# Instruction orders taken from a list schedule, five column blocks per ring, and block-diagonal kv weights, in an attention and channel-mix kernel

## The chip, the cores and the metric

The kernel runs on one core of a Trainium2 chip. The metric is the device time of one execution in microseconds (us), the median over repeated runs. A profiled execution also gives a span, from the first to the last instruction; where the record pairs the two, the span is about 1.7 to 2.1 us shorter than the time.

Engines are named as in the profile: PE is TensorE (PEld its weight loads), DVE is VectorE, ACT is ScalarE, POOL is GpSimd, SP is SyncE.

## The reference

There are 8 batches, 8 heads, 576 rows and head size 64. The attention has no score matrix: `exp(k)` is normalised over the sequence, `exp(q)` over the head size, and the kv matrix is 64 by 64 per head. The result goes into a channel mix with 1,024 hidden columns.

```python
q_s = exp(q - max);  q_s = q_s / sum(q_s, over head_dim)
k_s = exp(k - max);  k_s = k_s / sum(k_s, over seq)
x   = q_s @ (k_s.T @ v)                  # per head, then [batch, seq, 512]
x_prev = x shifted by one row
xk = mu_k*x + (1-mu_k)*x_prev;  xr = mu_r*x + (1-mu_r)*x_prev
out = sigmoid(xr @ w_r) * (relu(xk @ w_k)**2 @ w_v)
```

## The kernel before

Work comes in 16 attention groups (a batch and half of its heads) and in units of the channel mix. A group needs three loads of 576 KB (q, k, v), three operations on ScalarE, a row sum and a scaling of q on VectorE, kv products, nine transposes and two x products on TensorE, and then `xk` and `xr` on VectorE. A unit multiplies up to 512 columns of `xk` and `xr` by the weights. The kernel works in pairs of batches, with three units per pair, and mixes the two kinds of work by a rule that counts columns:

```python
UNITS = ((0, 512), (512, 384), (896, 256))           # per pair of batches
...
first = emit_load(0, 0, (nc.sync, nc.scalar, nc.sync))   # q, k, v of group 0
...                                                      # then the two small mu loads on nc.sync
emit_load(0, 1, (nc.scalar, nc.sync, nc.scalar))         # q, k, v of group 1
emit_weights(first[2])      # weight loads on GpSimd wait for group 0's v
...
def weights(self):                                   # kv weights of one group
    for hf in range(2):
        nc.vector.reciprocal(out=rz[:, hf:hf + 1], in_=self.kvp[hf][:, 128:129])
    for hf in range(2):                              # 128 x 128, off-diagonal blocks masked away
        nc.vector.scalar_tensor_tensor(
            out=self.w[:, hf, :], in0=self.kvp[hf][:, 0:128],
            scalar=rz[:, hf:hf + 1], in1=mask[:], op0=ALU.mult, op1=ALU.mult)
...
for pair in range(B // 2):
    for c0, n in UNITS:
        advance(ASTEPS * (2 * pair + (c0 + n - 1) // S))
        for c in unit(pair, c0, n, 4 if pair == 0 and c0 == 0 else 1):
            cols += c
            advance(min((B - 1) * ASTEPS, ASTEPS * (cols + per_batch // 8) // per_batch))
```

The softmax here doesn't subtract the row's maximum and nothing guards it: scores larger than these inputs give would overflow.

## Time and profile before

| | before |
|---|---|
| time, median (range) of three runs | 221.07 us (221.0 to 221.58) |
| profiled span | 219.7 us |
| matmul work, counted at the start-to-start time of back-to-back matmuls at full granted clock | 181.5 us |
| dense matmuls start | 27.8 us |
| TensorE time lost from there (27.8–40, 40–60, 60–160, from 160) | 1.9 + 2.9 + 4.7 + 1.0 us |
| tail after the last matmul | 4.75 us |

The work row is not the profile's busy time. In this trace matmuls of 512 columns start 0.216 us apart, and the 144 of L284 have a mean recorded duration of 0.379, so their records overlap. So matmuls are counted here by their start-to-start time (0.216 us at 512 columns), and "lost" is the stretch minus that work. "Warm" in the prediction means that rate: from 27.7 to 31.1 us, where this trace has a granted clock of 0.50, matmuls of 512 columns start 0.427 us apart.

The first lines are from the page of before: busy times, the span in 40 slices of 5.5 us (busy tenths; PEclk is the granted clock in tenths), and the chain of work that ended last, by engine.

```profile
PE 193.5 (88%) x1313; PEld 101.6 (46%) x1313; DVE 166.3 (76%) x384; ACT 147.7 (67%) x230; POOL 35.8 (16%) x56
...
PE   0156599988999999999999999999999999999991
...
DVE  1196389999999998889798998888787758483431
ACT  2645279999977779676929696949736392644340
...
PE 60%; ACT 19%; DVE 13%; DMA 3%; issue 2%; SPq 1%; DVEq 0%; ACTq 0%
```

TensorE is dense from about the sixth slice. VectorE is full up to about 85 us and ScalarE up to 60. The table of windows says it in numbers (columns: window, its length, then busy us and number of instructions of PE, PEld, DVE, ACT, POOL, then granted clock, DMA share and GB/s):

```profile
40.00:60.00 20.00, 18.34 (x141) 9.58 (x140) 19.93 (x45) 20.00 (x29) 8.31 (x12) 1.00 1.03 400
60.00:80.00 20.00, 19.92 (x140) 10.71 (x139) 19.79 (x46) 15.16 (x26) 4.95 (x7) 1.00 0.94 348
80.00:100.00 20.00, 19.41 (x121) 9.28 (x120) 17.39 (x36) 15.31 (x22) 4.24 (x6) 1.00 0.71 242
100.00:120.00 20.00, 19.81 (x161) 11.82 (x159) 17.52 (x42) 15.46 (x27) 2.12 (x3) 1.00 0.54 186
```

After 80 us VectorE has over 2 us free in each window of 20.

The head, from the timeline of before (columns: start, duration, engine, line, operation, output and inputs, count, and in brackets the idle time before it and what ended it):

```profile
5.97 2.22 ACT L154 ACTIVATE eqk<-raw 128x1152 bf16<-128x1152 f32 x2 [2.17 <-DMA raw<-in_q_dram]
...
9.79 0.24 PE L134 MATMUL mup<-identf,mu_sb 8*128 8x8 f32 x1 [9.79 <-DMA mu_sb<-in_moe_mu_r_dram]
...
10.16 1.34 DVE L166 TENSOR_REDUCE rsum<-eqk 128x18 f32<-128x1152 bf16 x1
...
13.25 1.14 PE L202 MATMUL qtp<-ident,qs 128*128 128x128 bf16 x9 [1.52 <-DVE qs L170]
...
27.82 1.01 PE L270 MATMUL kfp<-xk,wk_bf 128*128 128x512 bf16 x2 [2.92 <-DVE xk L232]
```

The first q has landed at 5.97 us, but its row sum starts only at 10.16. In the order of VectorE's instructions the copy of mu stands in front of it, and that copy starts at 10.07, after VectorE has been idle for 8.52 us: it waits for the transpose at 9.79, which waits for the small mu load.

### The profile page before, as it was taken

Reading aid. Unit: us, or ns where it says so; the run is one execution under the profiler, and the core shown is the slowest. Engines: PE = TensorE matmul, PEld = TensorE weight load, DVE = VectorE, ACT = ScalarE, POOL = GpSimd, SP = SyncE. Lnnn points to the kernel's source line nnn. Section 1 sums busy time; section 2 is a strip of 40 time slices with the busy share of each in tenths; the row PEclk is TensorE's granted clock in tenths of the full one; section 3 lists DMA queues with packets and bytes.
Section 4 is the critical chain, followed back from the end, with each engine's and each line's share of the span. In section 5 each row is a group of like instructions: output and inputs, shape, how many; then the busy total and the mean of one; then the engine's idle time right before and its main releaser. Section 6 shows DMA issues by size and latency. Waiting matters only on the chain.

```text
span 219.7 us, 3641 instructions
## 1 busy us (share of the span) xinstructions
PE 193.5 (88%) x1313; PEld 101.6 (46%) x1313; DVE 166.3 (76%) x384; ACT 147.7 (67%) x230; POOL 35.8 (16%) x56
## 2 busy tenths in 40 slices
PE   0156599988999999999999999999999999999991
PEld 0134134534547454445557443546465444554650
DVE  1196389999999998889798998888787758483431
ACT  2645279999977779676929696949736392644340
POOL 1294252433431210230030000000000000000000
PEclk9999969999999999999999999999999999999999
DMA  6999999999999791897085220232131400340414
GB/s 215 397 158 199 262 402 388 393 400 403 404 393 406 273 343 71 256 298 288 3 264 201 49 51 0 57 90 48 36 88 24 95 3 22 73 95 5 108 36 95
DMA packets 16171, 40.62 MB, mean 185 GB/s; under 512 B 2072, under 2 KB 4632, under 8 KB 16152
## 3 DMA queue, kind: packets, MB, share of 16 engines
q0 software_dynamic: 8736, 27.40, 38.0%
q1 hardware_dynamic: 6600, 11.22, 18.0%
q10 hardware_dynamic: 816, 1.77, 2.2%
q8 instruction: 10, 0.16, 0.3%
q14 instruction: 9, 0.07, 0.1%
HBM read 33.56 MB, written 9.44 MB: 196 GB/s over the span
## 4 chain that ended last, share of the span: by engine, by line
PE 60%; ACT 19%; DVE 13%; DMA 3%; issue 2%; SPq 1%; DVEq 0%; ACTq 0%
PE vp L291 22%; PE kfp L270 19%; PE rp L284 11%; ACT eqk L154 5%; ACT qt L207 4%; ACT rel L276 4%; DMA mu_sb<-in_moe_mu_r_dram 3%; PE kvp L184 3%; PE qtp L202 3%; PE xp L212 2%; DVE rsum L166 2%; DVE xk L232 2%; DVE qs L170 2%; ACT xb_105 L215 2%; ACT xb_109 L215 1%
## 5 line engine op out<-in xcount | busy, mean ns | idle before, releaser
L270 PE MATMUL kfp<-xk,wk_bf 128*128 128x384 bf16 (+2 forms) x384 | 72.6, 335 | 4.3 <-DVE xk L232 3.7
L276 ACT ACTIVATE rel<-kfp 128x512 bf16<-128x512 f32 (+2 forms) x96 | 45.4, 518 | 20.5 <-PE kfp L270 19.5
L270 PEld LDWEIGHTS <-wk_bf 128*128 128x128 bf16 x384 | 36.3, 99 | 30.3 <-issue 8.5
L154 ACT ACTIVATE eqk<-raw 128x1152 bf16<-128x1152 f32 x32 | 37.5, 1204 | 9.7 <-DMA raw<-in_q_dram 5.9
L294 DVE SCALAR_TENSOR_TENSOR ot<-th,vp 128x512 f32<-128x512 f32 x36 | 24.6, 683 | 17.3 <-PE vp L291 12.5
L287 ACT ACTIVATE th<-rp 128x512 f32<-128x512 f32 x36 | 22.7, 631 | 21.7 <-PE rp L284 20.7
L284 PE MATMUL rp<-wr_bf,xr 128*128 128x512 bf16 x144 | 37.0, 379 | 0.0
L207 ACT COPY qt<-qtp 128x1152 bf16<-128x1152 bf16 x16 | 18.2, 1136 | 7.7 <-PE qtp L202 7.5
L166 DVE TENSOR_REDUCE rsum<-eqk 128x18 f32<-128x1152 bf16 x16 | 21.6, 1348 | 1.6 <-ACT eqk L154 1.5
L170 DVE TENSOR_TENSOR qs<-eqk,rrec 128x1152 bf16<-128x1152 bf16 x16 | 21.7, 1355 | 0.8
L230 DVE TENSOR_SCALAR xm<-xd,mu 128x576 bf16<-128x576 bf16 x64 | 21.6, 378 | 0.4
L284 PEld LDWEIGHTS <-xr 128*128 128x128 bf16 x144 | 13.3, 98 | 13.8
L72 POOL DMA_DIRECT2D raw<-in_q_dram x14 | 10.0, 713 | 52.9 <-ACT vv_111 L160 24.0
L212 PE MATMUL xp<-qt,w 128*128 128x512 bf16 x64 | 13.5, 302 | 2.6 <-ACT qt L207 2.3
L184 PEld LDWEIGHTS <-eqk 64*128 64x128 bf16 x288 | 9.4, 100 | 9.2 <-issue 8.3
L202 PE MATMUL qtp<-ident,qs 128*128 128x128 bf16 x144 | 11.6, 231 | 1.5 <-DVE qs L170 1.5
L202 PEld LDWEIGHTS <-qs 128*128 128x128 bf16 x144 | 9.8, 103 | 4.1 <-DVE qs L170 1.8
L212 PEld LDWEIGHTS <-w 128*128 128x128 bf16 x64 | 6.3, 103 | 11.0 <-issue 6.1
L72 POOL DMA_DIRECT2D raw<-in_v_dram x14 | 10.0, 711 | 8.4 <-DMA raw<-in_q_dram 5.8
L72 POOL DMA_DIRECT2D raw<-in_k_dram x14 | 10.0, 711 | 5.7 <-DMA raw<-in_v_dram 3.0
L195 DVE SCALAR_TENSOR_TENSOR w<-kvp,rz,mask 128x128 bf16<-128x128 f32 x32 | 9.7, 345 | 0.0
L134 PE MATMUL mup<-identf,mu_sb 8*128 8x8 f32 x1 | 0.2, 243 | 9.8 <-DMA mu_sb<-in_moe_mu_r_dram 9.8
(83 smaller groups left out, 238.7 us busy)
## 6 DMA issues: line engine op xcount, KB each, us to landing
out_dram<-ot SPq DMA_DIRECT2D x72, 128.0 KB, 2.4
raw<-in_q_dram POOLq DMA_DIRECT2D x14, 576.0 KB, 12.4
raw<-in_k_dram POOLq DMA_DIRECT2D x14, 576.0 KB, 12.7
raw<-in_v_dram POOLq DMA_DIRECT2D x14, 576.0 KB, 13.1
wk_bf<-in_moe_w_k_dram POOLq DMA_DIRECT2D x4, 256.0 KB, 6.5
wv_bf<-in_moe_w_v_dram POOLq DMA_DIRECT2D x2, 512.0 KB, 12.4
raw<-in_k_dram ACTq DMA_DIRECT2D x1, 576.0 KB, 5.6
raw<-in_q_dram SPq DMA_DIRECT2D x1, 576.0 KB, 5.2
```

The costliest lines, as they stand in the source:

```text
L72: ld.append(queue.dma_start(out=t[:, i, :, :], in_=ap))
L154: nc.scalar.activation(out=self.eqk[:, i, :, :, :], in_=self.t[:, i, :, :].rearrange("p u (j d) -> p j u d", d=D), func=ACT.Exp)
L166: nc.vector.reduce_sum(out=rsum[:], in_=eq, axis=AX.X)
L170: nc.vector.tensor_tensor(out=self.qs[:].rearrange("p j (u d) -> p (j u) d", u=2), in0=eq, in1=rrec[:, :, None].to_broadcast((128, 2 * J, ...
L202: nc.tensor.transpose(out=self.qtp[:, j, :], in_=self.qs[:, j, :], identity=ident[:])
L207: nc.scalar.copy(out=self.qt[:], in_=self.qtp[:, 0:J, :])
L212: nc.tensor.matmul(self.xp[:, 64 * c:64 * e], lhsT=self.w[:, hf, :], rhs=self.qt[:, c:e, 64 * hf:64 * hf + 64], start=True, stop=True)
L270: nc.tensor.matmul(kfp[:, 0:n], lhsT=wk_bf[:, ct, fc * 128:(fc + 1) * 128], rhs=xk[:, ct, c0:c0 + n], start=(ct == 0), stop=(ct == CT - 1))
L276: nc.scalar.activation(out=rel[:, 0:n], in_=kfp[:, 0:n], func=ACT.Relu, scale=HALF_ROOT)
L284: nc.tensor.matmul(rp[:], lhsT=xr[:, ct, c0 + 128 * m:c0 + 128 * m + 128], rhs=wr_bf[:, ct, :], start=(ct == 0), stop=(ct == CT - 1))
L291: nc.tensor.matmul(vp[:], lhsT=k2[:, ft, 128 * m:128 * m + 128], rhs=wv_bf[:, ft, :], start=(ft == 0), stop=(ft == FT - 1))
L294: nc.vector.scalar_tensor_tensor(out=ot[:], in0=th[:], scalar=1.0, in1=vp[:], op0=ALU.add, op1=ALU.mult)
```

## The change

The intent is to replace the hand-made mixing rule by a schedule. Every operation is registered with its engine, the time that it occupies the engine (`occ`), its latency (`lat`), a priority key, its inputs and the buffers it takes and gives. A list scheduler then goes through them in simulated time, and the kernel emits each engine's instructions in the order of that plan. Four batches share a ring of 2,304 columns cut into five units instead of six, and the kv weights are written as two 64-partition diagonal blocks into a zeroed tile.

```diff
-    UNITS = ((0, 512), (512, 384), (896, 256))                       # per 2 batches
+    UNITS = ((0, 512), (512, 512), (1024, 512), (1536, 512), (2048, 256))   # per 4 batches
...
+class Plan:
+    def order(self):
+        while left:                       # simulated time, all engines
+            ...
+                    rank = (max(t, now + 0.03), op.key)      # t: when op could start
+            ...
+            if op.size:                   # loads: one stream of 395 KB/us
+                dma_free = max(dma_free, t + DMA_LEAD) + op.size / DMA_RATE
+                op.end = dma_free + DMA_TAIL
...
-    first = emit_load(0, 0, (nc.sync, nc.scalar, nc.sync)) ... mu ... emit_load(0, 1, ...)
-    emit_weights(first[2])                                   # weights wait for the first v
+    first = [load("SP", 0, 0, 0, 0), load("ACT", 0, 0, 1, 0), ...]
+    mu_load = plan.add("SP", 0.8, 0.8, 2, emit_mu_load, size=4.0)
+    wk_done.append(plan.add("POOL", 1.25, 1.25, h, ..., [], size=1048.0))    # no wait
...
-            for hf in range(2): nc.vector.reciprocal(...)            # 2 reciprocals
-            for hf in range(2): nc.vector.scalar_tensor_tensor(... in1=mask[:] ...)
+        def recz():                                                  # 1 reciprocal
+            nc.vector.reciprocal(out=rzs[w.index][:, :, None], in_=atts[kvp.index][:, :, 128:129])
+        def weights():
+            for u in range(2):
+                r = slice(64 * u, 64 * u + 64)
+                nc.vector.tensor_tensor(
+                    out=ws[w.index][r, :, r], in0=atts[kvp.index][r, :, r],
+                    in1=rzs[w.index][r, :, None].to_broadcast((64, 2, 64)), op=ALU.mult)
...
+        o = plan.add("DVE", 0.066, 0.15, step + 4, recz, [kvm], [w])
+        wdone = plan.add("DVE", 0.5, 0.6, step + 4, weights, [o], [], [kvp])
...
+    for op in plan.order():
+        op.emit()
```

In the resulting order the SyncE queue issues the mu loads first, then the first group's q. The first weight loads on GpSimd wait for nothing.

## The prediction

> **What bounds the kernel now.** TensorE, counted by work, not busy time. In the timeline, warm back-to-back matmuls start every 0.216 us at 512 columns, 0.163 at 384, 0.109 at 256; 18 kv products take 0.63 us, nine transposes 0.50. [...] Summed over all matmuls it is 181.5 us of the 219.7 us span. Lost, by 20 us windows of start times: 17.6 us before 20, 7.1 in 20-40, 2.9 in 40-60, 5.7 from 60 to 215, and 4.5 in the tail (last output operation and store). So 25 us are lost before dense matmuls run (27.8 us and shortly after); at most 8.6 can be won after 40.
>
> **What the change does.**
> 1. TensorE work stays: ten K units cost 62.2 us against 62.4.
> 2. VectorE: kv weights go from two reciprocals and two masked operations (0.84 us per group in the timeline) to one reciprocal and two 64-partition blocks, estimated 0.65: 3 us in 16 groups; fewer squares: 1 us. Off the critical path except in 40-80, where VectorE is 99% busy.
> 3. Body: ScalarE is busy 20.0 of 20 us in 40-60 while TensorE waits for its copies; the new orders spread this. Loss after 40 us: from 8.6 to about 4.
> 4. Head, better: mu loads go first. Before, mu landed at 9.65 us and held the first row sum until 10.16, though its exponential was done by 7.1.
> 5. Head, worse: the weight loads on the GpSimd queue no longer wait for the first v, so they start near 2.8 us and compete with the six first loads. By packets in the trace, the two hardware queues move about 85 each per us alone; in 11-12 us, when the weights join, the three move 64, 61 and 49[...]. At 60 packets per us a 256-packet load takes 4.3 us, not 3. Estimate: first q at 7.1 us (5.97 before), second group's q at 11.5, last of the six near 16 (12.7 before). ScalarE now takes the second group's q before the first's, so it waits to 11.5. Walking the new order with the old durations: first row sum 12.8, first xk 27, second xk 32, so dense matmuls begin at 30-32 us instead of 27.8: plus 2 to 4. Weights land 3 us earlier, batch 1's first q at 28 instead of 28.95.
>
> **Sum.** 31 us head + 176.5 remaining matmul work + 2 lost in the first unit + 2.5 later + 4.5 tail = 216.5 us. Predicted 216.5 us, 8 in 10 between 211.5 and 221. Faster by over 2% 0.47, within 2% 0.48, slower 0.05.
>
> **What would show it.** In the chain of waits and the timeline: the first row sum at 12-13 us, waiting for a DMA through ScalarE's exponential; dense K matmuls from 30-32 us; under 1 us lost per 20 us window after 60; the same last 4.5 us; weight packets from about 3 us, the six first loads landing by 16. VectorE busy falls by 3-6 us, with no effect of its own.
>
> **What would make it wrong.** If the weights do not slow the first loads, dense work starts at 27-28 us and the time is 211-213. If the fixed order meets waits that its durations did not foresee (two attention PSUM slots), the body keeps its losses and the time stays at 220.

31 + 176.5 + 2 + 2.5 + 4.5 is 216.5 us. The 0.216, 0.163 and 0.109 us, and the 64, 61 and 49 packets, are from the trace of before; that three queues would move 60 each for longer is the estimate from the latter. The 0.65 us of the new kv weights is a forecast of a form that had not run yet; in after it took 0.695 us from start to start.

## The result

After ran in 224.09 us (224.05 to 224.81, four runs), before in 221.03 us on the same chip (four runs, the three above and one more). The ratio is 1.0133, with a 95% interval of 1.0108 to 1.0159. A ratio here is the mean time of one kernel's fast runs over that of the other's in the same rounds, so it is not quite the ratio of the medians. The prediction's range ended at 221; the change costs 1.3%.

| | before | predicted | after |
|---|---|---|---|
| dense matmuls start | 27.8 | 31 | 30.2 |
| matmul work from there | 176.6 | 176.5 | 176.2 |
| TensorE time lost from there | 10.6 | 2 + 2.5 | 11.0 (1.5 before 40, 4.0 in 40–60, 5.3 in 60–160, 0.1 later) |
| tail | 4.75 | 4.5 | 4.75 |
| span | 219.7 | | 222.1 |
| time (before: its median; after: that run) | 221.07 | 216.5 | 224.11 |

Against before, the span is 2.4 us longer, and dense matmuls start 2.4 us later. From there on after loses 0.4 us more and has 0.4 us less to do. So the head cost about what it was expected to cost (partly by luck, as told below), and the gain that was expected of the body did not come. The granted clock is no rival: its mean was 0.990 in the profile of before and 1.000 in that of after.

The page of after, the same parts:

```profile
PE 190.5 (86%) x1249; PEld 95.2 (43%) x1249; DVE 159.7 (72%) x350; ACT 147.5 (66%) x214; POOL 35.9 (16%) x56
...
PE   0036569996799899999999989999999999999991
...
DVE  1271798999999999999999999999432442342431
ACT  4357259999999998999996662783452362372340
...
PE 54%; DVE 35%; DMA 4%; issue 3%; ACT 2%; SPq 0%; DVEq 0%
```

VectorE has 6.6 us less to do, and yet its share of the chain rose from 13% to 35%. The row of tenths says why: the list schedule takes attention work as early as it can, so VectorE shows nines without a gap until slice 28 (about 155 us) and ones to fours after that. In the windows:

```profile
40.00:60.00 20.00, 16.85 (x138) 8.32 (x137) 19.48 (x39) 20.00 (x26) 8.50 (x12) 1.00 1.04 401
60.00:80.00 20.00, 19.38 (x160) 10.15 (x159) 19.85 (x45) 20.00 (x28) 5.71 (x9) 1.00 1.03 384
80.00:100.00 20.00, 19.63 (x136) 9.34 (x134) 19.85 (x44) 19.38 (x27) 4.26 (x6) 1.00 0.85 291
100.00:120.00 20.00, 19.22 (x136) 9.44 (x134) 19.88 (x44) 18.62 (x26) 0.00 (x0) 1.00 0.17 38
```

The side engines are full where before had room. What TensorE waits for after 60 us in after (columns: waiting engine, tile and line, what it waits for, us in total, times, longest):

```profile
PE att_a L364 <- DVE w_b L344: 1.2, 2, 0.7
PE att_a L332 <- DVE w_b L344: 0.6, 1, 0.6
PE att_b L364 <- DVE w_b L344: 0.5, 1, 0.5
```

All of these, and the three smaller ones of that list, wait for VectorE's kv weights. Before has no wait on the kv weights in its list for the same stretch. In 38–60 us the list of after has three waits, of which these are the first two:

```profile
PE att_a L332 <- ACT vv_c L310: 1.6, 1, 1.6
PE att_b L364 <- DVE w_a L344: 0.8, 1, 0.8
```

The first is on ScalarE's cast of v, the second and the third (0.7 us) on the kv weights.

The head of after, in the timeline:

```profile
4.95 0.24 PE L252 MATMUL mm_a<-identf,mu_sb 8*128 8x8 f32 x1 [4.95 <-DMA mu_sb<-in_moe_mu_r_dram]
...
7.88 1.35 DVE L315 TENSOR_REDUCE rsum_a<-eq_a 128x18 f32<-128x1152 bf16 x1 [2.48 <-ACT eq_a L305]
9.27 0.27 DVE L320 RECIPROCAL rrec_a<-rsum_a 128x18 f32<-128x18 f32 x1
10.60 1.16 ACT L305 ACTIVATE eq_b<-raw_c 128x1152 bf16<-128x1152 f32 x1 [2.75 <-DMA raw_c<-in_q_dram]
...
11.79 1.35 DVE L315 TENSOR_REDUCE rsum_b<-eq_b 128x18 f32<-128x1152 bf16 x1 [2.26 <-ACT eq_b L305]
...
13.06 1.35 DVE L323 TENSOR_TENSOR qs_a<-eq_a,rrec_a 128x1152 bf16<-128x1152 bf16 x1
...
14.47 0.82 PE L353 MATMUL att_a<-ident,qs_a 128*128 128x128 bf16 x6 [9.28 <-DVE qs_a L323]
...
30.18 0.59 PE L454 MATMUL mm_b<-xk,wk_bf 128*128 128x512 bf16 x2 [1.34 <-DVE xk L387]
```

The first row sum is 2.3 us earlier than before, as intended. Then VectorE stops. `qs_a` (the second group's scaling) has all it needs at 9.54, but it stands behind `rsum_b`, which waits for the first group's q; and that q lands at 10.5. VectorE is idle for 2.26 us before `rsum_b` at 11.79, and `qs_a` starts at 13.06, 3.5 us after it could have. The chain of waits of after starts with that load (start, duration, what):

```profile
1.48 9.09 DMA raw_c<-in_q_dram
```

### A way to read a scheduled kernel

The kernel carries its own plan, so each instruction has a planned start. Running the scheduler alone gives the plan's end, and the trace gives the lag: chip start minus planned start, here of VectorE's instructions. Times beside a lag are times of the plan. The plan of after ends at 214.57 us. The lag is +3.9 us at 15 us, 3.7 at 40, 4.8 at 66, 5.8 at 91, 6.4 at 116 and 6.7 at the end. The plan's end plus the last lag plus 0.8 us of last store is 222.1, the span. So the loss has two parts: a step of 3.8 us at the head, and a creep of about 3 us between 40 and 135 us. Of the 2.6 us by which the lag grows between 40 and 140 us, 1.5 arise at the kv weights and their reciprocals; the rest is spread over the other kinds of instruction, under 0.6 us for each. The plan allows itself no idle time of TensorE or of VectorE from 60 to 120 us, so it cannot make up for a lag there.

### The profile page after: what moved, and what is told of

Read it like the earlier page. It is cut to its first block, busy times and chain, and to the rows that moved or that the text cites. A ratio compares the mean times of both kernels' runs of the same rounds, so it can differ in the third digit from the quotient of the medians.

```text
span 222.1 us, 3476 instructions
## 1 busy us (share of the span) xinstructions
PE 190.5 (86%) x1249; PEld 95.2 (43%) x1249; DVE 159.7 (72%) x350; ACT 147.5 (66%) x214; POOL 35.9 (16%) x56
## 4 chain that ended last, share of the span: by engine, by line
PE 54%; DVE 35%; DMA 4%; issue 3%; ACT 2%; SPq 0%; DVEq 0%
PE mm_a L495 6%; PE mm_d L495 6%; PE mm_b L485 5%; PE mm_c L495 5%; PE mm_a L454 5%; DMA raw_c<-in_q_dram 4%; PE mm_b L495 4%; PE mm_c L454 4%; PE mm_d L454 3%; DVE xk L387 3%; PE mm_c L485 3%; PE mm_b L454 3%; DVE qs_a L323 2%; PE mm_d L485 2%; DVE qs_b L323 2%
## 5 line engine op out<-in xcount | busy, mean ns | idle before, releaser
L454 PE MATMUL mm_a<-xk,wk_bf 128*128 128x512 bf16 (+1 forms) x100 | 24.3, 362 | 0.0
L454 PE MATMUL mm_c<-xk,wk_bf 128*128 128x512 bf16 (+1 forms) x80 | 19.6, 364 | 0.5 <-ACT rel_b L439 0.5
L495 PEld LDWEIGHTS <-k_a 128*128 128x128 bf16 x144 | 13.4, 97 | 15.4
L495 PEld LDWEIGHTS <-k_b 128*128 128x128 bf16 x144 | 13.2, 98 | 15.0
L454 PE MATMUL mm_d<-xk,wk_bf 128*128 128x512 bf16 (+1 forms) x80 | 19.6, 364 | 0.0
L454 PE MATMUL mm_b<-xk,wk_bf 128*128 128x512 bf16 (+1 forms) x60 | 14.5, 359 | 3.6 <-DVE xk L387 3.6
L485 PE MATMUL mm_b<-wr_bf,xr 128*128 128x512 bf16 x68 | 17.5, 379 | 0.0
L495 PE MATMUL mm_a<-wv_bf,k_a 128*128 128x512 bf16 x48 | 12.3, 379 | 0.0
L495 PE MATMUL mm_a<-wv_bf,k_b 128*128 128x512 bf16 x48 | 12.2, 379 | 0.0
L495 PE MATMUL mm_c<-wv_bf,k_b 128*128 128x512 bf16 x40 | 10.3, 379 | 0.0
## 6 DMA issues: line engine op xcount, KB each, us to landing
raw_l<-in_v_dram POOLq DMA_DIRECT2D x4, 576.0 KB, 10.5
```

Source lines behind the costliest of these rows:

```text
L454: nc.tensor.matmul(mms[kf.index][:, 0:n], lhsT=wk_bf[:, ct, fc * 128:(fc + 1) * 128], rhs=xs[0][:, ct, c0:c0 + n], start=(ct == 0), stop=( ...
L485: nc.tensor.matmul(mms[rps.index][:], lhsT=xs[1][:, ct, c:c + 128], rhs=wr_bf[:, ct, :], start=(ct == 0), stop=(ct == CT - 1))
L495: nc.tensor.matmul(mms[vps.index][:], lhsT=k2s[k2.index][:, ft, 128 * m:128 * m + 128], rhs=wv_bf[:, ft, :], start=(ft == 0), stop=(ft == ...
```

## The experiments

The head theory says that the late first q makes the whole program late. It has two causes to choose from: the two mu loads in front of it in its queue, or the weight loads that share the DMA engines. The body theory says that VectorE has more work than the plan's durations say, and that a full VectorE hands the difference to TensorE. Rivals to the latter are ScalarE, which is just as full in 40–80, and the five units. In the texts below, where a letter stands for a theory of the first runs, A is that of the head. Results first:

| run | time (before on the same chip) | ratio, 95% | plan ends | lag at 15 us | last lag | span |
|---|---|---|---|---|---|---|
| after | 224.09 (221.03) | 1.0133, 1.0108–1.0159 | 214.57 | 3.9 | 6.7 | 222.1 |
| e1_q_first | 226.07 (221.82) | 1.0203, 1.0182–1.0225 | 214.57 | 5.6 | 8.3 | 223.7 |
| e2_gate | 223.83 (221.82) | 1.0112, 1.0084–1.0140 | 214.57 | 2.15 | 6.3 | 221.7 |
| e3_half_rsum (wrong result) | 220.45 (221.82) | 0.9950, 0.9927–0.9972 | 214.57 | 3.2 | 3.45 | 218.9 |
| e4_masked | 222.90 (221.82) | 1.0065, 1.0043–1.0088 | 214.57 | 3.9 | 5.2 | 220.6 |
| e5_both_relief (wrong result) | 216.42 (221.60) | 0.9775, 0.9752–0.9797 | 214.57 | 2.5 | −0.8 | 214.6 |
| e6_six | 223.74 (221.60) | 1.0098, 1.0076–1.0121 | 214.51 | 4.0 | 6.8 | 222.2 |
| e7_replan | 217.86 (221.60) | 0.9832, 0.9812–0.9852 | 211.70 | 4.2 | 3.6 | 216.1 |
| e8_replan_lands | 216.06 (221.60) | 0.9755, 0.9731–0.9779 | 212.65 | −0.2 | 0.6 | 214.0 |
| e9_lands_only | 222.58 (221.60) | 1.0035, 1.0010–1.0060 | 214.59 | −0.1 | 5.2 | 220.7 |
| e10_blocks_dur | 218.25 (221.60) | 0.9849, 0.9823–0.9876 | 211.81 | 4.1 | 3.95 | 216.5 |
| e11_tie | 215.64 (221.60) | 0.9726, 0.9705–0.9747 | 211.99 | 0.6 | 0.95 | 213.8 |
| e12_gate_replan | 222.76 (221.60) | 1.0052, 1.0021–1.0082 | 216.03 | −0.1 | 3.9 | 220.7 |

In every row the span is the plan's end plus the last lag plus 0.7 to 0.9 us. So an edit can act in two ways: it can change what the plan promises, or how well the chip keeps it. The traces of e5 to e12 lack about 22 of 1,249 matmul records, so for them lost TensorE time is not summed finely; the lag of VectorE does not need those records.

### The head: queue order and weight loads

e1 issues the first q before the mu loads and keeps all orders otherwise.

```diff
-    for op in plan.order():
+    planned = plan.order()
+    planned.remove(mu_load)
+    planned.insert(planned.index(first[0]) + 1, mu_load)
+    for op in planned:
         op.emit()
```

> The changed kernel with one move: on the SyncE queue the first q goes before the two small mu loads instead of behind them; every other order is kept. Theory A (the mu loads at the head of that queue hold back the first q, whose packets start only at 5.0 us although it is issued at 1.48): the first q lands at 6 to 7.5 us instead of 10.5, the second group's q somewhat later than 6.7, dense matmuls (second xk) start at 26.5 to 28 instead of 30.2, and the time falls by 2.5 to 3.8 us from 224.1, to 220.3-221.6. Theory B (the first q is late because the weight loads share the DMA engines from 5 us on): it starts early but still shares, lands at 9 to 10, and the time falls by less than 1.5 us.

The queue did what was asked: packets of q start at 1.8 us instead of about 5. Yet the kernel became slower. In after, the ScalarE queue has 3 to 5 us almost alone (188 packets of it and 9 of SyncE's start in the us from 4), and brings k and the second group's q by 6.65. In e1 both queues share that time (66 and 67 packets in the us from 3), so k lands at 6.67 and the second q at 10.7, and ScalarE's order asks for these first. From the timeline of e1:

```profile
10.75 1.16 ACT L305 ACTIVATE eq_a<-raw_b 128x1152 bf16<-128x1152 f32 x1 [2.92 <-DMA raw_b<-in_q_dram]
...
14.73 1.34 DVE L323 TENSOR_TENSOR qs_a<-eq_a,rrec_a 128x1152 bf16<-128x1152 bf16 x1
```

So the head lag rose by 1.7 us. The mu loads do hold up the first q, but in this order of work that is no loss as such: what counts is which load lands before which instruction. The times that either theory had given were missed: both had the kernel become faster.

e2 lets the weights wait for the first v again, as before did.

```diff
-        nc.gpsimd.dma_start(out=dst[64 * u:64 * u + 64, :, c0:c1], in_=ap)
+        ld = nc.gpsimd.dma_start(out=dst[64 * u:64 * u + 64, :, c0:c1], in_=ap)
+        if "gated" not in issued:
+            tc.add_manual_dep(ld.ins, issued[0, 0, 2].ins.name, SYNC)
+            issued["gated"] = True
```

> The changed kernel with the weight loads held back until the first v has landed, as in the kernel before; mu stays first on its queue, all orders are kept. Theory A: the first q's packets still start at 5.0 us, but share with one other queue only, so it lands near 8 instead of 10.5; time falls by at most 2.5 us, and the later landing of batch 1 (first q of batch 1 near 29 instead of 27) gives up to 1 us back. Theory B: it lands at 6 to 7, and the time falls by 3 to 3.8 us.

The first q's exponential then starts at 8.84 us instead of 10.60, `qs_a` starts at 11.31 instead of 13.06, and the lag at 15 us falls to 2.15. But everything behind the weights comes later, batch 1's q among it. From ScalarE's waits in e2, 20–35 us:

```profile
ACT eq_c L310 <- DMA raw_g<-in_q_dram: 3.9, 1, 3.9
```

That exponential starts at 29.82 us instead of 27.36, and the lag is back at 3.6 by 37 us. Within the intervals, e2 is as slow as after. So the first q, with one queue less to share with, still came late: nearer to theory A's 8 us than to the 6 to 7 of theory B. Holding the weights back moved the wait to batch 1.

### The body: VectorE, ScalarE, blocks and units

e3 sums over 8 of 64 columns in every row sum. The result is wrong; 16 instructions of 1.33 us become 0.28 us.

```diff
-                                 in_=eqs[eq.index][:].rearrange("p j u d -> p (j u) d"),
+                                 in_=eqs[eq.index][:].rearrange("p j u d -> p (j u) d")[:, :, 0:8],
```

> The changed kernel with the row sums taken over 8 of 64 columns (wrong result on purpose): about 1 us of VectorE work less per group, 16 us in all, orders kept. Theory C (from 36 to 150 us VectorE has no idle time, and each delay there goes through the fixed orders to TensorE): TensorE's lost time from 60 to 160 us, 5.4 us now, falls under 1.5 us, the head also starts 1 to 2 us earlier, and the time falls by 5 to 8 us. Rival D (TensorE's body waits come from the fixed orders and the two attention PSUM slots, whatever VectorE's load): only the head's 1 to 2 us are won.

The time falls by 1.8% against after, less than the 5 to 8 us expected. The creep is gone (lag 3.2 at 15 us, 3.45 at the end), TensorE's list of waits after 60 us has none on VectorE, and its loss in 60–160 is 3.0 us instead of 5.3 (under 1.5 was expected). So the creep passes through VectorE: where VectorE has slack, there is none. The remaining 3.0 us have another cause. That it is the durations of the plan which make the creep is not shown by this run, but by e7 and e10 below.

e4 puts the old masked kv weights back, with the orders kept.

```diff
-            nc.vector.reciprocal(out=rzs[w.index][:, :, None],
-                                 in_=atts[kvp.index][:, :, 128:129])
+            for hf in range(2):
+                nc.vector.reciprocal(out=rzs[w.index][:, hf:hf + 1],
+                                     in_=atts[kvp.index][:, hf, 128:129])
...
-            for u in range(2):
-                r = slice(64 * u, 64 * u + 64)
-                nc.vector.tensor_tensor(
-                    out=ws[w.index][r, :, r], in0=atts[kvp.index][r, :, r], ...)
+            for hf in range(2):
+                nc.vector.scalar_tensor_tensor(
+                    out=ws[w.index][:, hf, :], in0=atts[kvp.index][:, hf, 0:128],
+                    scalar=rzs[w.index][:, hf:hf + 1], in1=mask[:],
+                    op0=ALU.mult, op1=ALU.mult)
```

> The changed kernel with the old form of the kv weights (two reciprocals and two masked 128x128 operations per group) in place of one reciprocal and two blocks; orders kept. What the prediction said of the blocks (0.15 us of VectorE per group, 3 us in all) with theory C gives plus 2 to 3 us. But from the traces one group takes 0.80 us before and 0.79 after from the first reciprocal's start to the last block's end: by that the time stays within 0.7 us of 224.1.

Undoing the cheaper form makes the kernel faster: the span falls by 1.5 us, and the creep from 2.8 to 1.3. Part of the reason is in the timeline. In after:

```profile
44.70 0.58 DVE L344 TENSOR_TENSOR w_b<-att_b,rz_b 64x128 bf16<-64x128 f32 x2
...
45.31 0.69 DVE L501 SCALAR_TENSOR_TENSOR ot_b<-th_b,mm_a 128x512 f32<-128x512 f32 x1
```

And the masked form, in e7:

```profile
45.05 0.60 DVE L346 SCALAR_TENSOR_TENSOR w_b<-att_b,rz_b,mask 128x128 bf16<-128x128 f32 x2
...
45.57 0.68 DVE L504 SCALAR_TENSOR_TENSOR ot_b<-th_b,mm_a 128x512 f32<-128x512 f32 x1
```

The masked pair has instructions of 0.34 us each that overlap, so the pair takes 0.60, and the next instruction starts about 0.08 us before its end. The blocks have 0.274 and 0.294 us, with no overlap inside the pair, and the next instruction starts 0.03 us after its end. Averaged over the groups and counted from start to start, the blocks take 0.614 us of VectorE's queue, the masked pair 0.520. With the reciprocals it is 0.695 against 0.664, while the plan had 0.566. The difference of 0.031 us makes 0.5 us in 16 groups, a third of what e4 gained. The rest came from other VectorE instructions: between 36 and 140 us of the plan, row sums, scalings and others followed each other 0.005 to 0.02 us faster than in after, 1.1 us in all. Why they did, no run shows. In 15 of the 16 groups of after the next instruction starts 0.03 us after the end of the blocks. Why nothing overlaps the blocks is not shown either: the two forms differ in operation, in the number of partitions and in where these start, and no run varied one of them alone. It does not show in the busy time, where the blocks have less (0.58 against 0.60 us).

e5 is e3 plus casts of v over 8 of 64 columns, to relieve ScalarE as well; the result is wrong.

```diff
             nc.scalar.copy(
-                out=vvs[vv.index][:, :, 0:128].rearrange("p j (u d) -> p j u d", u=2),
-                in_=raws[sv.index][:].rearrange("p u (j d) -> p j u d", d=D))
+                out=vvs[vv.index][:, :, 0:128].rearrange("p j (u d) -> p j u d", u=2)[:, :, :, 0:8],
+                in_=raws[sv.index][:].rearrange("p u (j d) -> p j u d", d=D)[:, :, :, 0:8])
```

> The run with short row sums (wrong result) and in addition the casts of v over 8 of 64 columns (still wrong on purpose): about 0.8 us less of ScalarE work per group, orders kept. The short row sums alone removed the creep of TensorE against its planned start times (3.3 us at 46, 3.5 at the end) but left 3.75 us lost in 40-60 us. Theory E (that rest is ScalarE, busy 20.0 of 20 us there): the loss in 40-60 falls under 2.5 us and the time is 1 to 2 us under that run's 220.5. Rival (it is in the fixed order itself, whose own planned TensorE idle there is 3.3 us): the loss stays above 3.2 us and the time within 0.7 us of 220.5.

It gains 4 us more than e3, and both expectations missed the time: the lag falls from 2.4 at 40 us of the plan to −0.5 at 91, a stretch where ScalarE is full in after. So with VectorE relieved, ScalarE is a limit there too. A run that relieves ScalarE alone was not made.

e6 keeps everything but cuts the ring into the old six units, and plans anew.

```diff
-    UNITS = ((0, 512), (512, 512), (1024, 512), (1536, 512), (2048, 256))
+    UNITS = ((0, 512), (512, 384), (896, 256), (1152, 512), (1664, 384), (2048, 256))
```

> The changed kernel with the old six units per four batches (512, 384 and 256 columns twice) instead of five; the schedule is made again by the same rule. TensorE's work is 0.2 us more, VectorE's and ScalarE's fixed costs 16 operations each more. If the number of units matters through those fixed costs on a saturated VectorE: plus 0.5 to 1.5 us on 224.1. If not (the units were chosen for earlier need of later batches): within 0.7 us either way.

The ratio is 1.0098 against 1.0133, with overlapping intervals: the number of units is not the cause. (The "fixed costs" of that text show in the trace of before: a square on VectorE takes 0.42 us at 512 columns and 0.29 at 256, a relu on ScalarE 0.62 and 0.40, so half the columns cost more than half the time.) The creep stays as well, 2.8 us, although the orders are new.

### The plan: durations and landings

e7 has the masked weights and gives the plan the start-to-start durations that the trace of after shows; the scheduler makes new orders.

```diff
-        o = plan.add("DVE", 0.066, 0.15, step + 4, recz, [kvm], [w])
-        wdone = plan.add("DVE", 0.5, 0.6, step + 4, weights, [o], [], [kvp])
+        o = plan.add("DVE", 0.142, 0.23, step + 4, recz, [kvm], [w])
+        wdone = plan.add("DVE", 0.52, 0.6, step + 4, weights, [o], [], [kvp])
...      # rsum 1.26 to 1.25, scale_q 1.262 to 1.27, diff and mix 0.66 to 0.67 and 0.668,
...      # scale_x 0.28 to 0.287, square +0.01, gated 0.593 to 0.604
```

> The changed kernel with masked kv weights, and the schedule made again with the VectorE durations that the traces of the changed kernel show (0.66 us per group for the masked weights, others 0.01 longer). Theory C (the body's creep is work that the schedule did not count on a VectorE without idle time): the creep of TensorE's starts against the new schedule from 45 to 150 us falls from 2.85 us (1.35 with masked weights) to under 0.7 us, and the time to 220-222.5. Rival: the creep stays, and the time with it near the masked run's 222.9.

It is faster than expected. The creep is gone (4.2 to 3.6), and the plan itself ends at 211.70 instead of 214.57, though no kind of work but the row sum became shorter in it: its planned loss of TensorE in 40–60 (idle time, and matmuls that the plan by its own rule counts at half speed after a pause) happened to fall from 3.3 to 0.5 us. A list schedule is not monotone, so that half of the gain is luck as far as these runs show.

e10 answers whether the masked form was needed: it is after itself with honest durations for the blocks.

```diff
-        o = plan.add("DVE", 0.066, 0.15, step + 4, recz, [kvm], [w])
-        wdone = plan.add("DVE", 0.5, 0.6, step + 4, weights, [o], [], [kvp])
+        o = plan.add("DVE", 0.17, 0.2, step + 4, recz, [kvm], [w])
+        wdone = plan.add("DVE", 0.6, 0.6, step + 4, weights, [o], [], [kvp])
...      # the other durations as in e7
```

> The changed kernel with its kv blocks and its old landing times; only the VectorE durations are told to the schedule as measured (0.77 us per group for the blocks). Against the same with masked weights (217.9, schedule's end 211.7) it has a schedule's end of 211.8. Theory C (uncounted VectorE work was the harm, not the blocks as such): the creep from 45 to 150 us is under 0.7 us and the time 217.3 to 218.8. Rival (the blocks themselves cost TensorE time): 219.3 or more.

This is the cleanest run: the instructions are those of after, in another order, and the time falls from 224.1 to 218.25 us, as expected. Of the 5.6 us in the span, 2.8 are the plan's earlier end, the same luck as in e7, and 2.8 the creep that went away. A new order alone does not remove the creep: e6 and, below, e9 are planned anew with the old durations and keep 2.8 us of it. Against e7 the blocks cost 0.4 us, which the intervals do not separate from nothing. So the blocks hurt mostly because the plan did not count them.

e8 is e7 and also tells the plan when the first loads really land, instead of one stream of 395 KB per us (the page of after has 391 to 409 GB/s in slices 6 to 13, and 205 to 311 in the five before).

```diff
+            if op in self.lands:
+                op.end = self.lands[op]
-            if op.size:
+            elif op.size:
...
+    for op, at in zip(first + [mu_load] + wk_done + [wr_done] + wv_done,
+                      (10.55, 4.6, 13.6, 6.65, 16.2, 12.1, 4.9, 13.3, 17.3, 19.7, 22.1, 24.6)):
+        plan.lands[op] = at
```

> As the last, and the schedule is also given the landing times of the first loads and weights as the trace shows them (first q 10.55 us, not 6.6; last of the six 16.2, not 13.8), so VectorE no longer places the second row sum before the first scaling. The head's order was made for landings that did not come: by that the first transposes start at 12 to 13 us instead of 14.5, the head wins 1 to 2 us, and the time is 218 to 221. Rival (the loads bound the head whatever the order): within 0.7 us of the run before it in this list.

Now the plan knows that the second group's q lands first and puts its scaling straight behind its row sum. From the timeline of e8:

```profile
7.90 1.35 DVE L320 TENSOR_REDUCE rsum_a<-eq_a 128x18 f32<-128x1152 bf16 x1 [2.41 <-ACT eq_a L310]
...
9.59 1.36 DVE L328 TENSOR_TENSOR qs_a<-eq_a,rrec_a 128x1152 bf16<-128x1152 bf16 x1
...
11.00 1.14 PE L359 MATMUL att_a<-ident,qs_a 128*128 128x128 bf16 x9 [5.71 <-DVE qs_a L328]
```

The q of the first group still lands near 10.9 us, but nothing stands behind it any more; the first transposes run at 11.0 instead of 14.47. The lag stays below 1.5 us to the end, and the time is 216.06 us, 1.8 below e7. A gain of 1 to 2 us was expected; the range of 218 to 221 was set before e7's time was known.

A further difference was read, and not tested alone. In after, VectorE does a second row sum of batch 2 before the last `xk` of batch 1, which the second unit needs:

```profile
50.81 1.34 DVE L315 TENSOR_REDUCE rsum_b<-eq_c 128x18 f32<-128x1152 bf16 x1
...
53.68 0.75 DVE L387 TENSOR_TENSOR xk<-xm_a,xb_b 128x1152 bf16<-128x1152 bf16 x1
```

In e8 the same `xk` comes first:

```profile
48.68 0.74 DVE L393 TENSOR_TENSOR xk<-xm_a,xb_b 128x1152 bf16<-128x1152 bf16 x1
...
50.90 1.34 DVE L328 TENSOR_TENSOR qs_a<-eq_b,rrec_a 128x1152 bf16<-128x1152 bf16 x1
```

TensorE is busy 19.47 us of 40–60 in e8, and 16.85 in after. That this row sum makes the difference is not shown. In after TensorE's list of waits for 38–60 names the cast of v and the kv weights, and not this `xk`. In e9 below TensorE does wait 2.0 us for it, although the second row sum of batch 2 stands behind it there.

e9 gives after the landings alone, with the old durations: the other half of e8.

> The changed kernel with its kv blocks and its old VectorE durations; only the landing times of the first loads and weights are told to the schedule as the trace shows them. The schedule's own end stays 214.6 us (with 3.4 us of planned TensorE idle in 40-60). Theory: the head's 3.8 us lag behind the schedule goes to about 0.6, the body's creep of 2.85 us stays, so the time is 4.1 us over the schedule's end plus the 2 us by which the timed runs exceed the profile's end: 219.5 to 221.5. Rival (the head is bound by the loads, the order gives nothing): 223 to 224.5.

The head lag is gone at 15 us (−0.1), but it is 2.4 us at 40 and 5.2 at the end. The expectation of 219.5 to 221.5 us was missed by 1.1. From 40 us on the creep is that of after, 2.8 us, as expected. The 2.4 us before that are lost at the head, while VectorE still has pauses: 1.4 of them come between 29 and 33 us of the plan, in the first unit. The unit's matmuls of 512 columns start at 25.3 us in e9 and in e8, at first 0.43 us apart and later 0.22. The change comes at about 30.8 us in e9 and 28.2 in e8; the first record of a granted full clock in these traces is at 31.1 us and at 28.5. Why it came 2.6 us later in e9 is not shown, and the timed runs do not tell whether it did so in all of them. So e9 shows that the landings without the durations leave the creep; its full distance from e8 is not the worth of the durations alone. By the ratios, landings alone gain 1.0% on after (e9), durations alone 2.8% (e10), and both, with the masked weights, 3.7% (e8).

e11 is e8 with one edit of the scheduler's rule for ties: it no longer treats operations that are ready within 0.03 us as equally early.

```diff
-                    rank = (max(t, now + 0.03), op.key)
+                    rank = (max(t, now), op.key)
```

> As the fastest run so far (masked weights, measured VectorE durations and landing times; 216.06 us, schedule's end 212.65), with the rule for ties changed: an operation that can start at once goes by priority only, not with any that can start within 0.03 us. The schedule's end is 211.99. If the chip follows a schedule that counts right, to within 0.7 us: 214.9 to 216.1. If such differences of the schedule are below what the chip keeps: 216 or more.

It gave the lowest time, 215.64 us (215.34 to 215.73), as expected: 2.7% below before, and by the two ratios (0.9726 over 1.0133) 4% below after. From e8 it is not clearly separated, because the intervals overlap. It is correct and may replace both kernels.

e12 is e8 with the weights waiting for the first v, and a plan that knows the landings of that case.

> As the fastest run so far, with the weight loads held back until the first v has landed and the schedule made again for the landings that the gated run showed (first q 8.8 us, last of the six 11.9, weights to 26.9, batch 1's first q 29.7). What the prediction took for a loss (weights competing with the first loads) is undone here with an order that can use it. If early weights were a net loss: below 215.5. If holding them back only moves the wait to batch 1, whose loads then land 2.5 us later (planned TensorE idle in 40-60: 8.1 us): 217.5 to 220.

It is 6.7 us slower than e8, and 2.8 us over the upper expectation. Its head is early, but batch 1 lands late, and TensorE runs dry in 40–60, with its clock granted at 0.74; the lag grows from 1.3 to 4.3 us between 40 and 66 us of the plan. From the windows of e12:

```profile
40.00:60.00 20.00, 11.06 (x100) 6.43 (x101) 17.93 (x39) 18.49 (x21) 8.38 (x13) 0.74 1.04 402
```

So early weights, which the prediction took for a cost of the head, are worth keeping once the order fits them, as far as this one order with late weights shows.

## Why the prediction was wrong

1. **What bounds the kernel.** Right as bookkeeping: start of dense work, work, losses and tail add up to the span in both kernels. But the prediction looked at TensorE's losses and not at how much room the engines that feed it would have. From 60 us on before loses 5.7 us with VectorE at about 17.4 of 20 us in 80–140; after loses 5.4 with VectorE at 19.9.
2. **VectorE saves 3 us in the kv weights, "off the critical path except in 40-80".** The busy time did fall, from 166.3 to 159.7 us, a little more than the 3 to 6 expected. In the queue the blocks save nothing: 0.614 us from start to start against 0.520 for the masked pair. And the new order fills VectorE from 40 to 140 us, so they are on the critical path there; e4 shows 1.5 us, a third of it by their own time in the queue.
3. **"Loss after 40 us: from 8.6 to about 4."** This is the step that failed. It measured 9.4 us (4.0 in 40–60, 5.3 in 60–160, 0.1 later). With the stretch before 40, the sum's "2 lost in the first unit + 2.5 later" measured 11.0. The prediction took a planned order for one that is carried out. It said that the new orders would spread ScalarE's work, but ScalarE is busy 20.0 of 20 us in 40–60 as before, and now in 60–80 too, and the longest wait of TensorE in 38–60 is for its cast of v (1.6 us). The plan itself had 3.3 us of TensorE loss in 40–60, then none, and its VectorE durations for the kv weights were 0.13 us per group too short with no slack to absorb it. The claim "under 1 us lost per 20 us window after 60" was wrong as well: 1.1, 1.2, 1.2, 1.0 and 0.8 us up to 160, and almost none later. e7 and e10 remove the creep by honest durations, e3 by slack.
4. **Head, better.** Half right. Mu landed at 4.95 instead of 9.65 us, and the first row sum came at 7.88 instead of 10.16. But the mu loads held the q behind them: issued at 1.48, its packets started at about 5, after those of the two mu loads (1.7 to 2.0 us, and 3.9 to 4.3). Why the second came so late, and the q after it, the traces do not show.
5. **Head, worse.** The estimate of 60 packets per us was right: 51 to 62 on each of three queues in 7–10 us. Who lands first was the wrong way round (second q at 6.65, first at 10.5; predicted 11.5 and 7.1), because two things were missed: the first q stood behind the mu loads, and so the ScalarE queue was alone at 3 to 5 us. The weights, expected near 3 us, sent their first packets at 5.6. The sum was right by luck, 30.2 us for 30 to 32. Batch 1's first exponential started at 27.36 (28 predicted), and the last first load landed near 16 as predicted.
6. **Span and time.** The sum was of spans, and it was given as a time. The timed run is 2.0 us longer than its span (224.11 and 222.1). For before the record does not say which run was profiled; it is between 1.3 and 1.9.

The terms together, against 216.5: head −0.8, work −0.3, losses +6.5, tail +0.25 and span to time +2.0, which gives 224.15. The last sentence of the prediction named the danger, a fixed order that meets waits its durations did not foresee, as one of two ways to be wrong. It was the main case, although the waits were for VectorE's weights and for a load, not for the PSUM slots that it names.

What stays open: how much of the 4.0 us lost in 40–60 belongs to the place of one row sum before `xk`, which was read and not tested alone; why the loss of about 3 us in 60–160 remains without creep; why two thirds of e4's gain came from instructions that it did not change; and why full clock came later in e9.

## What to carry to other kernels

A static order computed from durations was here only as good as the start-to-start time of each instruction in its queue and the landing time of each load: compare the plan's start of each instruction with the trace's, and look for a step (a load, a wait) and for a creep (a duration). VectorE, which the greedy schedule filled to 99%, passed such errors on here, so a saving in instructions on such an engine has to be measured from start to start, not as busy time (e4: 0.614 against 0.520 us from start to start, with 0.58 against 0.60 us busy). Correct the durations and landings together and plan anew before judging the parts of such a change: here the same instructions went from 1.3% slower to 1.5% faster when only the durations in the plan were changed, half by a creep that went away and half by a plan that happened to end earlier.
